# Decode attention with whole-load VectorE instructions: one multiply, half-add and sum per 8 MB K load, and 512-byte aligned buffers

## The chip, the cores and the metric

One core of one Trainium2 chip. The metric is the device time of one execution in microseconds (us), taken as the median of several executions. The span of a profile is about 2 us shorter than the device time. PE is TensorE, DVE VectorE, ACT ScalarE, SP the engine that issues the loads.

## The reference, cut to what matters

Two problems of the same form, A and B: one new token, 32 heads of 128, K and V caches of 16,384 keys. A attends to all keys, B to the last 4,096.

```python
q = (x @ wq).reshape(B, Sq, Hq, Dh)                  # Sq = 1, Hq = Hkv = 32, Dh = 128
scores = einsum("bhqd,bhkd->bhqk", q, k) * Dh**-0.5  # B: k and v are the last 4096 keys
p = softmax(scores); o = einsum("bhqk,bhkd->bhqd", p, v)
return o.reshape(B, Sq, Hq * Dh) @ wo                # the two results are concatenated
```

In bf16 this reads 268 MB of K and V for A, 67 MB for B and 16.8 MB of weights, 352 MB in all, for very little arithmetic.

## The kernel before: the parts that matter

K and V are read in 20 loads of 8 MB each (16 of A, 4 of B, one B load after every four of A). Each of the 128 partitions gets 256 consecutive keys of one head, 64 KB. There are two buffers for K and one for V; all loads are issued in one fixed order (K0, K1, V0, K2, V1, ...), each as soon as its buffer is free. An A load is one "unit" of two heads; a B load is two units of four heads each.

A load of K is worked on in two chunks of 128 keys. DVE multiplies K by q in place, adds the upper half of each key's 128 products to the lower half, PE sums the 64 rest to 8 with matmuls by the identity into PSUM, DVE sums those 8, ACT takes the exp:

```python
def _mult(nc, cx, ch):
    k = u.load.kt[:, ch.k0 : ch.k0 + U, :]                       # U = 128 keys
    cx.o(nc.vector.tensor_tensor(out=k, in0=k, in1=q..., op=ALU.mult))
def _add(nc, cx, ch):
    cx.o(nc.vector.tensor_tensor(out=k[:, :, 0:64], in0=k[:, :, 0:64], in1=k[:, :, 64:128], op=ALU.add))
def _red(nc, cx, ch):                                            # 16 matmuls, 2 PSUM banks
    ch.red = cx.red_pool.tile([P, U, W], F32, tag="red")         # red_pool: 2 buffers
    ...
def _softmax(nc, cx, ch):                                        # DVE sum of 8, then R exps on ACT
    ...
```

P·V runs on PE, one unit at a time, into one of two PSUM accumulators. Then DVE "picks" the wanted rows (a masked multiply, L247, and a sum, L253), and PE folds them into the result. The order in which this is put into the engines' programs (`...` marks cuts):

```python
    def pv(load):
        for u in load.units:
            fin_pe()                   # PE: fold units already picked
            fin_dve()                  # DVE: pick units whose P.V has been issued
            _pv(nc, cx, u)             # PE: P.V
            ...
    for i, x in enumerate(loads):
        for c, ch in enumerate(x.chunks):
            _mult(nc, cx, ch)
            if prev is not None:
                _softmax(nc, cx, prev)
            fin_pe()
            _add(nc, cx, ch)
            fin_dve()
            _red(nc, cx, ch)
            if i and c == 0:
                pv(loads[i - 1])       # P.V of the load before
            prev = ch
```

At the end the output weights wo (8 MB) are loaded into V's buffer, in pieces of which B's last are small, and PE multiplies: 32 matmuls for A, 64 narrower ones for B (`out_ps`).

The 64 KB buffers of this kernel start 256 bytes past a multiple of 512, since the small tiles lie below them.

The softmax here doesn't subtract the row's maximum and nothing guards it: scores larger than these inputs give would overflow.

Of the kernel before, what the change touches and what calls it, by code (L numbers as in the profile page):

```python
# [10 lines left out]
P = 128  # L11
# [4 lines left out]
DH = 128  # L16
U = 128
W = 8
KEYS = 256
# [42 lines left out]

class _Chunk:
    def __init__(self, unit, i):
        self.unit, self.i, self.k0 = unit, i, unit.k0 + i * U


class _Unit:


    def __init__(self, st, i, load, k0):
        self.st, self.i, self.R = st, i, st.R
        self.load, self.k0 = load, k0
        self.h0 = i * st.R
        self.chunks = [_Chunk(self, c) for c in range(st.keys // U)]
        self.stage = None


class _Load:


    def __init__(self, st, i):
        self.st = st
        n = KEYS // st.keys
        self.units = [_Unit(st, i * n + j, self, j * st.keys) for j in range(n)]
        self.chunks = [ch for u in self.units for ch in u.chunks]

# [39 lines left out]
def _q(nc, cx, st):  # L127

    D, N = st.wq.shape
    KC = D // P  # L130
    R = st.R
    n = N // R
    st.qall = cx.singles.tile([P, n], BF16, tag=f"qall{st.name}", name=f"qall{st.name}")
    for j in range(n // 512):
        q_ps = cx.red_pool.tile([P, 512], F32, tag="red", name="q_ps")
        for g in range(R):
            for c in range(KC):
                w = st.wq_t[:, c, :].rearrange("p (u g d) -> p g u d", g=R, d=DH)
                cx.o(nc.tensor.matmul(  # L139
                    q_ps[:, :],  # L140
                    lhsT=st.xb[:, c, g, :],
                    rhs=w[:, g, j * (512 // DH) : (j + 1) * (512 // DH), :],
                    start=(g == 0 and c == 0),
                    stop=(g == R - 1 and c == KC - 1),
                ))
        cx.o(nc.scalar.copy(st.qall[:, j * 512 : (j + 1) * 512], q_ps[:, :]))

# [21 lines left out]

def _mult(nc, cx, ch):  # L170

    u = ch.unit
    k = u.load.kt[:, ch.k0 : ch.k0 + U, :]
    q = u.st.qall[:, u.i * DH : (u.i + 1) * DH]
    cx.o(nc.vector.tensor_tensor(  # L175
        out=k, in0=k,
        in1=q.rearrange("p (o d) -> p o d", o=1).broadcast_to([P, U, DH]),
        op=ALU.mult,
    ))


def _add(nc, cx, ch):
    k = ch.unit.load.kt[:, ch.k0 : ch.k0 + U, :]
    cx.o(nc.vector.tensor_tensor(  # L184
        out=k[:, :, 0 : DH // 2], in0=k[:, :, 0 : DH // 2], in1=k[:, :, DH // 2 : DH], op=ALU.add,
    ))


def _red(nc, cx, ch):
    n = 512 // W  # L190
    nb = DH // 2 // W
    ch.red = cx.red_pool.tile([P, U, W], F32, tag="red", name="red")
    for k in range(0, U, n):
        for b in range(nb):
            cx.o(nc.tensor.matmul(  # L195
                ch.red[:, k : k + n, :],
                lhsT=cx.ident[:, :],
                rhs=ch.unit.load.kt[:, ch.k0 + k : ch.k0 + k + n, b * W : (b + 1) * W],
                start=(b == 0),
                stop=(b == nb - 1),  # L200
            ))
    if ch is ch.unit.load.chunks[-1]:
        cx.loads.release("kt")


def _softmax(nc, cx, ch):

    u = ch.unit
    R = u.R
    sc = cx.sc_pool.tile([P, U], F32, tag="sc", name="sc")  # L210
    cx.o(nc.vector.tensor_reduce(out=sc[:, :], in_=ch.red[:, :, :], axis=AX.X, op=ALU.add))  # L211
    ch.p = u.st.p_pool.tile([P, U // 4, R, 4], BF16, tag=f"p{u.st.name}", name="p_sb")
    for g in range(R):
        cx.o(nc.scalar.activation(  # L214
            out=ch.p[:, :, g, :],
            in_=sc[:, :].rearrange("p (t e) -> p t e", e=4),
            func=ACT.Exp,
            scale=SCALE,
            bias=u.st.off[:, g : g + 1],
            accum_out=u.st.cs[:, u.h0 + g, ch.i : ch.i + 1],  # L220
        ))


def _pv(nc, cx, u):

    R = u.R
    cx.turn = 1 - cx.turn
    u.acc = cx.acc[cx.turn]
    T = u.st.keys // 4
    for t in range(T):  # L230
        r = 32 * (t % 4)
        ch, k = u.chunks[4 * t // U], u.k0 + 4 * t
        cx.o(nc.tensor.matmul(  # L233
            u.acc[r : r + 4 * R, :],
            lhsT=ch.p[:, t % (U // 4), :, :],
            rhs=u.load.vt[:, k : k + 4, :],
            start=(t < 4),
            stop=(t >= T - 4),
        ))
    if u is u.load.units[-1]:  # L240
        cx.loads.release(u.load.v_tag)


def _fin_pick(nc, cx, u):
# [6 lines left out]
    ))  # L251
    u.s = cx.small.tile([P, DH], F32, tag="s", name="s")
    cx.o(nc.vector.tensor_reduce(  # L253
# [15 lines left out]
def _fin_rows(nc, cx, sts):  # L269
    H = 32  # L270
    csum = cx.small.tile([P, 2 * H], F32, tag="csum", name="csum")
    for st in sts:
        cx.o(nc.vector.tensor_reduce(
            out=csum[:, st.f_at : st.f_at + H], in_=st.cs[:, :, :], axis=AX.X, op=ALU.add,
        ))
        cx.o(nc.tensor.matmul(
            cx.f_ps[st.f_at : st.f_at + H, DH : DH + 1],
            lhsT=csum[:, st.f_at : st.f_at + H], rhs=cx.ones_col[:, 0:1],
            start=False, stop=True, skip_group_check=True,
        ))  # L280
# [48 lines left out]
def kernel(  # L329
# [22 lines left out]
    pool = lambda name, bufs, **kw: ctx.enter_context(tc.tile_pool(name=name, bufs=bufs, **kw))  # L352
    PS = dict(space=bass.MemoryType.PSUM)
    cx.singles = pool("singles", 1)
    cx.small = pool("small", 1)
    cx.kt_pool = pool("kt", 2)
    cx.vt_pool = pool("vt", 1)
    cx.accs_pool = pool("accs", 1)
    cx.sc_pool = pool("sc", 1)
    cx.p_poolA = pool("pA", 3)  # L360
    cx.p_poolB = pool("pB", 2)
    cx.red_pool = pool("red", 2, **PS)
    cx.psf_pool = pool("psf", 1, **PS)
# [7 lines left out]
    def problem(name, x, k_cache, v_cache, wq, wo, sk0, W, at):  # L371
# [10 lines left out]
        assert k_cache.shape[1] == 32  # L382
        st.p_pool = cx.p_poolA if name == "A" else cx.p_poolB
        n = KEYS // st.keys * st.R
# [34 lines left out]
    at = (stA.R + stB.R) * (A_wq.shape[0] // P) * P  # L419
    cx.one = cx.singles.tile([1, 1], BF16, tag="one", name="one")  # L420
    nc.gpsimd.memset(cx.one[:, :], 1.0)

    cx.ones_col = cx.singles.tile([P, 1], F32, tag="ones_col", name="ones_col")
    nc.gpsimd.memset(cx.ones_col[:, :], 1.0)
    ones = cx.scr[:, at : at + 3 * P]
    nc.gpsimd.memset(ones, 1.0)
    cx.ident = cx.singles.tile([P, P], BF16, tag="ident", name="ident")
    nc.gpsimd.affine_select(
# [21 lines left out]
    )  # L450

    rows = cx.small.tile([P, 32], F32, tag="rows", name="rows")
    nc.vector.tensor_reduce(
        out=rows[:, :], in_=cx.ident[:, :].rearrange("p (c w) -> p w c", w=32), axis=AX.X, op=ALU.add,
    )
    for st in (stA, stB):
        H, R = 32, st.R
        st.cs = cx.singles.tile([P, H, st.keys // U], F32, tag=f"cs{st.name}", name=f"cs{st.name}")
        own = rows[:, 0 : 4 * R].rearrange("p (g e) -> p g e", e=4)
# [11 lines left out]
    for st in (stA, stB):  # L471
        st.off = cx.singles.tile([P, st.R], F32, tag=f"off{st.name}", name=f"off{st.name}")
        nc.vector.tensor_reduce(
            out=st.off[:, :],
            in_=cx.ident[:, :].rearrange("p (i g) -> p g i", g=st.R),
            axis=AX.X,
            op=ALU.add,
        )
        nc.vector.tensor_scalar(
            out=st.off[:, :], in0=st.off[:, :], scalar1=-1.0, scalar2=1000.0,  # L480
            op0=ALU.add, op1=ALU.mult,
        )
# [17 lines left out]

    fins = []

    def fin_pe():
        for u in fins:
            if u.stage == 1:
                _fin_fold(nc, cx, u)
                u.stage = 9
        fins[:] = [u for u in fins if u.stage != 9]

    def fin_dve():  # L510
        for u in fins:
            if u.stage == 0:
                _fin_pick(nc, cx, u)
                u.stage = 1

    def pv(load):
        for u in load.units:
            fin_pe()
            fin_dve()
            _pv(nc, cx, u)  # L520
            u.stage = 0
            fins.append(u)

    prev = None
    for i, x in enumerate(loads):
        for c, ch in enumerate(x.chunks):
            _mult(nc, cx, ch)
            if prev is not None:
                _softmax(nc, cx, prev)
            fin_pe()  # L530
            _add(nc, cx, ch)
            fin_dve()
            _red(nc, cx, ch)
            if i and c == 0:
                pv(loads[i - 1])
            prev = ch
    _softmax(nc, cx, prev)
    fin_pe()
    fin_dve()
    pv(loads[-1])  # L540
    while fins:
        fin_pe()
        fin_dve()
    _fin_rows(nc, cx, (stA, stB))
# [32 lines left out]
```

## Time and profile before

| | before |
|---|---|
| device time, median of 3 | 823.35 us (823.29 to 824.57) |
| span of the profile | 821.3 us |
| share of 16 DMA engines' span used by the load queue | 99.3% |
| DVE busy, PE busy | 603.5 us (73%), 341.5 us (42%) |

These lines are from the page of the kernel before: busy time of the engines, GB/s moved in 40 slices of the span, the packets and the load queue.

```profile
PE 341.5 (42%) x2148; PEld 127.6 (16%) x2148; DVE 603.5 (73%) x196; ACT 46.8 (6%) x201; POOL 1.3 (0%) x9
...
GB/s 385 436 457 409 456 413 453 411 452 421 427 442 444 425 440 428 437 419 447 421 444 437 431 435 434 432 422 444 440 418 451 425 444 421 445 415 454 413 423 321
DMA packets 8238, 352.65 MB, mean 429 GB/s; under 512 B 916, under 2 KB 920, under 8 KB 1304
...
q1 hardware_dynamic: 8212, 352.33, 99.3%
```

No slice between the first and the last drops: the swings between 409 and 457 come from the bookkeeping, which counts a 64 KB packet whole in the slice in which it starts; by the starts and ends of the packet records no 10 us between 10 and 810 us has engine time lost. The records have a median of 2.418 us per 64 KB packet, 27.1 GB/s per engine and 434 GB/s for 16.

The next view is the chain of waits that ended last, cut to the end of the span (start, length, what). Each line is what released the next.

```profile
756.14 42.58 DMA vt<-in_B_v_cache_dram
...
798.77 3.49 PE acc L233 x31
...
805.50 8.70 PE out_ps L313 x32
...
815.05 3.70 PE out_ps L313 x64
818.75 0.41 DVE rowB L322
```

After the last V has landed, the end is reached through PE's work, not through the wo load. Yet the last packet of wo also lands only at 818.0 us by the packet records: the two end together.

The timeline of SP near the start shows when loads are issued (start, length of the issue):

```profile
75.75 0.54 SPq L167 DMA_DIRECT2D kt<-in_A_k_cache_dram  x1
93.19 0.54 SPq L167 DMA_DIRECT2D vt<-in_A_v_cache_dram  x1
103.48 0.54 SPq L167 DMA_DIRECT2D kt<-in_A_k_cache_dram  x1
124.50 0.53 SPq L167 DMA_DIRECT2D vt<-in_A_v_cache_dram  x1
```

The first line is K2. The loads issued before it (wq, K0, K1, V0) are 33.6 MB, which at 434 GB/s from 1.8 us on last to about 79 us.

### The profile page before, as it was taken

How to read it: one execution, taken by the hardware profiler on the slowest of the kernel's cores; microseconds unless marked ns; L12 is line 12 of the kernel's file. 1: busy time of each engine (PE TensorE's matmuls, PEld its weight loads, DVE VectorE, ACT ScalarE, POOL GpSimd, SP SyncE). 2: the span in 40 equal slices, each digit the busy share in tenths (PEclk: the TensorE clock that was granted, in tenths of full speed). 3: DMA queues.
4: the chain of work that ended last, by engine and by line, in shares of the span. 5: the costliest groups of instructions: out<-in, count | busy, mean ns of one | idle time of the engine just before them, and what ended most of it. 6: DMA issues, size and time to landing. Idle time of an engine off the chain costs nothing.

```text
span 821.3 us, 4921 instructions
## 1 busy us (share of the span) xinstructions
PE 341.5 (42%) x2148; PEld 127.6 (16%) x2148; DVE 603.5 (73%) x196; ACT 46.8 (6%) x201; POOL 1.3 (0%) x9
## 2 busy tenths in 40 slices
PE   3433743435043517162433524344504360715267
PEld 1111211112011202021111211111201120202123
DVE  2099895996469967799169959599556987689911
ACT  1100000000000000001000000000000000000100
POOL 0000000000000000000000000000000000000000
PEclk9856678667676756686757776777767576758678
DMA  9999999999999999999999999999999999999997
GB/s 385 436 457 409 456 413 453 411 452 421 427 442 444 425 440 428 437 419 447 421 444 437 431 435 434 432 422 444 440 418 451 425 444 421 445 415 454 413 423 321
DMA packets 8238, 352.65 MB, mean 429 GB/s; under 512 B 916, under 2 KB 920, under 8 KB 1304
## 3 DMA queue, kind: packets, MB, share of 16 engines
q1 hardware_dynamic: 8212, 352.33, 99.3%
q8 instruction: 17, 0.28, 0.1%
q14 instruction: 5, 0.04, 0.0%
q10 hardware_dynamic: 4, 0.00, 0.0%
HBM read 352.32 MB, written 0.00 MB: 429 GB/s over the span
## 4 chain that ended last, share of the span: by engine, by line
DMA 54%; DVE 22%; PE 15%; issue 8%; SPq 0%; ACT 0%; DVEq 0%
DMA kt<-in_A_k_cache_dram 41%; PE red L195 11%; DVE kt L184 10%; DMA vt<-in_A_v_cache_dram 9%; DVE kt L175 8%; DMA vt<-in_B_v_cache_dram 5%; DVE sc L211 2%; PE acc L233 2%; PE out_ps L313 2%; DVE s L253 0%; DVE acc L247 0%; SPq L124 0%; DVE rowA L322 0%; SPq L167 0%; DVE rowB L322 0%
## 5 line engine op out<-in xcount | busy, mean ns | idle before, releaser
L195 PE MATMUL red<-kt,ident 128*128 128x512 bf16 x640 | 223.3, 526 | 417.7 <-DVE kt L184 417.7
L175 DVE TENSOR_TENSOR kt<-kt,qallA 128x16384 bf16<-128x16384 bf16 x32 | 278.0, 8686 | 135.1 <-DMA kt<-in_A_k_cache_dram 135.1
L184 DVE TENSOR_TENSOR kt<-kt 128x8192 bf16<-128x8192 bf16 x40 | 176.5, 4413 | 0.0
L195 PEld LDWEIGHTS <-ident 128*128 128x128 bf16 x640 | 79.0, 129 | 557.2 <-DVE kt L184 404.8
L233 PE MATMUL acc<-vt,p_sb 128*8 128x512 bf16 (+1 forms) x1280 | 83.0, 416 | 43.0 <-DMA vt<-in_A_v_cache_dram 35.5
L175 DVE TENSOR_TENSOR kt<-kt,qallB 128x16384 bf16<-128x16384 bf16 x8 | 69.5, 8682 | 0.0
L214 ACT ACTIVATE p_sb<-sc,offA 128x128 bf16<-128x128 f32 x64 | 25.2, 394 | 556.8 <-DVE sc L211 556.8
L211 DVE TENSOR_REDUCE sc<-red 128x128 f32<-128x1024 f32 x40 | 48.7, 1216 | 2.2 <-PE red L195 2.2
L233 PEld LDWEIGHTS <-p_sb 128*8 128x8 bf16 (+1 forms) x1280 | 32.3, 93 | 91.8 <-issue 63.0
L247 DVE TENSOR_TENSOR acc<-acc,maskB 128x512 f32<-128x512 f32 x8 | 5.6, 696 | 33.7 <-PE acc L233 33.7
L247 DVE TENSOR_TENSOR acc<-acc,maskA 128x512 f32<-128x512 f32 x16 | 11.1, 692 | 24.9 <-PE acc L233 24.9
L214 ACT ACTIVATE p_sb<-sc,offB 128x128 bf16<-128x128 f32 x32 | 12.4, 390 | 163.7 <-DVE sc L211 163.7
L139 PE MATMUL q_ps<-wq_t,scr 128*128 128x512 bf16 x64 | 16.0, 413 | 5.4 <-DMA wq_t<-in_A_wq_dram 4.8
L253 DVE TENSOR_REDUCE s<-acc 128x128 f32<-128x512 f32 x24 | 16.6, 691 | 1.1
L214 ACT ACTIVATION_READ_ACCUMULATOR p_sb<-sc,offA 128x1 f32 x64 | 11.9, 186 | 0.0
L313 PE MATMUL out_ps<-wo_t,ocA 128*1 128x512 bf16 x32 | 8.7, 438 | 0.3 <-DVE ocA L306 0.3
L139 PEld LDWEIGHTS <-scr 128*128 128x128 bf16 x64 | 6.5, 104 | 14.5 <-issue 7.3
L322 DVE CAST rowA<-out_ps 1x512 bf16<-1x512 f32 x1 | 0.7, 679 | 8.8 <-PE out_ps L313 8.8
L261 PE MATMUL f_ps<-s,selA 128*32 128x128 f32 x32 | 6.5, 285 | 0.0
L214 ACT ACTIVATION_READ_ACCUMULATOR p_sb<-sc,offB 128x1 f32 x32 | 6.0, 186 | 0.0
L111 DVE CAST scr<-xT 128x128 bf16<-128x128 f32 (+1 forms) x6 | 2.1, 460 | 3.8 <-PE xT L103 3.7
L313 PE MATMUL out_ps<-wo_t,ocB 128*1 128x256 bf16 x64 | 3.7, 272 | 0.9 <-DVE ocB L306 0.9
(45 smaller groups left out, 27.5 us busy)
## 6 DMA issues: line engine op xcount, KB each, us to landing
kt<-in_B_k_cache_dram SPq DMA_DIRECT2D x8, 4096.0 KB, 33.2
vt<-in_B_v_cache_dram SPq DMA_DIRECT2D x8, 4096.0 KB, 23.4
wq_t<-in_A_wq_dram SPq DMA_DIRECT2D x1, 4096.0 KB, 12.2
wq_t<-in_B_wq_dram SPq DMA_DIRECT2D x1, 4096.0 KB
wo_t<-in_A_wo_dram SPq DMA_DIRECT2D x2, 2048.0 KB, 22.3
wo_t<-in_B_wo_dram SPq DMA_DIRECT2D x1, 2048.0 KB, 26.6
wo_t<-in_B_wo_dram SPq DMA_DIRECT2D x1, 1024.0 KB, 28.7
wo_t<-in_B_wo_dram SPq DMA_DIRECT2D x1, 512.0 KB
```

The source lines that it names most:

```text
L111: cx.o(nc.vector.tensor_copy(st.xb[:, :, g, :].rearrange("p c (i r) -> p r c i", r=R)[:, g, :, :], xT[:, :].rearrange("p (c o) -> p c o", ...
L139: cx.o(nc.tensor.matmul(q_ps[:, :], lhsT=st.xb[:, c, g, :], rhs=w[:, g, j * (512 // DH) : (j + 1) * (512 // DH), :], start=(g == 0 and c = ...
L175: cx.o(nc.vector.tensor_tensor(out=k, in0=k, in1=q.rearrange("p (o d) -> p o d", o=1).broadcast_to([P, U, DH]), op=ALU.mult,))
L184: cx.o(nc.vector.tensor_tensor(out=k[:, :, 0 : DH // 2], in0=k[:, :, 0 : DH // 2], in1=k[:, :, DH // 2 : DH], op=ALU.add,))
L195: cx.o(nc.tensor.matmul(ch.red[:, k : k + n, :], lhsT=cx.ident[:, :], rhs=ch.unit.load.kt[:, ch.k0 + k : ch.k0 + k + n, b * W : (b + 1) * ...
L211: cx.o(nc.vector.tensor_reduce(out=sc[:, :], in_=ch.red[:, :, :], axis=AX.X, op=ALU.add))
L214: cx.o(nc.scalar.activation(out=ch.p[:, :, g, :], in_=sc[:, :].rearrange("p (t e) -> p t e", e=4), func=ACT.Exp, scale=SCALE, bias=u.st.of ...
L233: cx.o(nc.tensor.matmul(u.acc[r : r + 4 * R, :], lhsT=ch.p[:, t % (U // 4), :, :], rhs=u.load.vt[:, k : k + 4, :], start=(t < 4), stop=(t ...
L247: cx.o(nc.vector.tensor_tensor(out=acc, in0=acc, in1=st.mask[:, :].rearrange("p (x o) -> p x o", o=1).broadcast_to([P, 4, DH]), op=ALU.mult,))
L253: cx.o(nc.vector.tensor_reduce(out=u.s[:, :], in_=acc.rearrange("p x d -> p d x"), axis=AX.X, op=ALU.add,))
L261: cx.o(nc.tensor.matmul(cx.f_ps[st.f_at : st.f_at + 32, 0:DH], lhsT=st.sel[:, at : at + 32], rhs=u.s[:, :], start=(u.i == 0), stop=(u.i == ...
L313: cx.o(nc.tensor.matmul(out[x], lhsT=st.oc[:, j : j + 1], rhs=st.wo_t[:, j, x * w : (x + 1) * w], start=(j == 0), stop=(j == J - 1),))
```

## The change

The intent: fewer and longer DVE and ACT instructions, a simpler order, and K and V buffers on multiples of 512 bytes. A whole K load is multiplied in one instruction (two for B, whose two units have their own q), half-added in one and summed in one; its sums fill four PSUM banks with a single buffer. Only the first two loads are worked on in parts (four and two). A's exps cover 256 keys. Small tiles that must lie low stay below the big buffers, and the rest goes above. The picks of a load now come after both of its P·V units. Core of the diff, cut:

```diff
-def _mult(nc, cx, ch):
+def _mult(nc, cx, load, k0, k1):
+    for u in load.units:
+        a, b = max(k0, u.k0), min(k1, u.k0 + u.st.keys)
...
-    ch.red = cx.red_pool.tile([P, U, W], F32, tag="red", name="red")
+    if k0 == 0:
+        load.red = cx.red_pool.tile([P, KEYS, W], F32, tag="red", name="red")
...
-    cx.singles = pool("singles", 1)
-    cx.small = pool("small", 1)
+    cx.low = pool("low", 1)
     cx.kt_pool = pool("kt", 2)
     cx.vt_pool = pool("vt", 1)
+    cx.singles = pool("singles", 1)
+    cx.small = pool("small", 1)
+    cx.s_pool = pool("s", 2)
...
-    cx.red_pool = pool("red", 2, **PS)
+    cx.red_pool = pool("red", 1, **PS)
...
-    def pv(load):
-        for u in load.units:
-            fin_pe()
-            fin_dve()
-            _pv(nc, cx, u)
...
+    def end(load):
+        for u in load.units:
+            _fin_pick(nc, cx, u)
+        for u in load.units:
+            _fin_fold(nc, cx, u)
...
+        n = KEYS // (4, 2)[i] if i < 2 else KEYS
+        for k in range(0, KEYS, n):
+            _mult(nc, cx, x, k, k + n)
+            if prev is not None and k == 0:
+                _softmax(nc, cx, prev)
+            _add(nc, cx, x, k, k + n)
+            if prev is not None and k == 0:
+                for u in prev.units:
+                    _pv(nc, cx, u)
+            _red(nc, cx, x, k, k + n)
+        if prev is not None:
+            end(prev)
```

More of the change, by code (lines that the diff above doesn't have):

```diff
@@ L16 @@
 DH = 128
-U = 128
 W = 8
@@ L60, in pump @@
             fn()
-class _Chunk:
-    def __init__(self, unit, i):
-        self.unit, self.i, self.k0 = unit, i, unit.k0 + i * U
 class _Unit:
@@ L74, in __init__ @@
         self.h0 = i * st.R
-        self.chunks = [_Chunk(self, c) for c in range(st.keys // U)]
-        self.stage = None
 class _Load:
@@ L85, in __init__ @@
         self.units = [_Unit(st, i * n + j, self, j * st.keys) for j in range(n)]
-        self.chunks = [ch for u in self.units for ch in u.chunks]
 def _load_x(nc, cx, st, w):
@@ L133, in _q @@
     st.qall = cx.singles.tile([P, n], BF16, tag=f"qall{st.name}", name=f"qall{st.name}")
+    q_ps = cx.red_pool.tile([P, n // 512, 512], F32, tag="red", name="q_ps")
     for j in range(n // 512):
-        q_ps = cx.red_pool.tile([P, 512], F32, tag="red", name="q_ps")
         for g in range(R):
@@ L139, in _q @@
                 cx.o(nc.tensor.matmul(
-                    q_ps[:, :],
+                    q_ps[:, j, :],
                     lhsT=st.xb[:, c, g, :],
@@ L145, in _q @@
                 ))
-        cx.o(nc.scalar.copy(st.qall[:, j * 512 : (j + 1) * 512], q_ps[:, :]))
+    cx.o(nc.scalar.copy(st.qall[:, :], q_ps[:, :, :].rearrange("p j f -> p (j f)")))
 def _load_wo(nc, cx, st, j0, n):
@@ L167, in _load_kv, with _add @@
         cx.o(nc.sync.dma_start(out=t[:, u.k0 : u.k0 + st.keys, :], in_=src))
-def _mult(nc, cx, ch):
-    u = ch.unit
-    k = u.load.kt[:, ch.k0 : ch.k0 + U, :]
-    q = u.st.qall[:, u.i * DH : (u.i + 1) * DH]
-    cx.o(nc.vector.tensor_tensor(
-        out=k, in0=k,
-        in1=q.rearrange("p (o d) -> p o d", o=1).broadcast_to([P, U, DH]),
-        op=ALU.mult,
-    ))
-def _add(nc, cx, ch):
-    k = ch.unit.load.kt[:, ch.k0 : ch.k0 + U, :]
+def _mult(nc, cx, load, k0, k1):
+    for u in load.units:
+        a, b = max(k0, u.k0), min(k1, u.k0 + u.st.keys)
+        if a >= b:
+            continue
+        k = load.kt[:, a:b, :]
+        q = u.st.qall[:, u.i * DH : (u.i + 1) * DH]
+        cx.o(nc.vector.tensor_tensor(
+            out=k, in0=k,
+            in1=q.rearrange("p (o d) -> p o d", o=1).broadcast_to([P, b - a, DH]),
+            op=ALU.mult,
+        ))
+def _add(nc, cx, load, k0, k1):
+    k = load.kt[:, k0:k1, :]
     cx.o(nc.vector.tensor_tensor(
@@ L186, in _add, with _red @@
     ))
-def _red(nc, cx, ch):
+def _red(nc, cx, load, k0, k1):
     n = 512 // W
     nb = DH // 2 // W
-    ch.red = cx.red_pool.tile([P, U, W], F32, tag="red", name="red")
-    for k in range(0, U, n):
+    if k0 == 0:
+        load.red = cx.red_pool.tile([P, KEYS, W], F32, tag="red", name="red")
+    for k in range(k0, k1, n):
         for b in range(nb):
             cx.o(nc.tensor.matmul(
-                ch.red[:, k : k + n, :],
+                load.red[:, k : k + n, :],
                 lhsT=cx.ident[:, :],
-                rhs=ch.unit.load.kt[:, ch.k0 + k : ch.k0 + k + n, b * W : (b + 1) * W],
+                rhs=load.kt[:, k : k + n, b * W : (b + 1) * W],
                 start=(b == 0),
@@ L201, in _red, with _softmax @@
             ))
-    if ch is ch.unit.load.chunks[-1]:
+    if k1 == KEYS:
         cx.loads.release("kt")
-def _softmax(nc, cx, ch):
-    u = ch.unit
-    R = u.R
-    sc = cx.sc_pool.tile([P, U], F32, tag="sc", name="sc")
-    cx.o(nc.vector.tensor_reduce(out=sc[:, :], in_=ch.red[:, :, :], axis=AX.X, op=ALU.add))
-    ch.p = u.st.p_pool.tile([P, U // 4, R, 4], BF16, tag=f"p{u.st.name}", name="p_sb")
-    for g in range(R):
-        cx.o(nc.scalar.activation(
-            out=ch.p[:, :, g, :],
-            in_=sc[:, :].rearrange("p (t e) -> p t e", e=4),
-            func=ACT.Exp,
-            scale=SCALE,
-            bias=u.st.off[:, g : g + 1],
-            accum_out=u.st.cs[:, u.h0 + g, ch.i : ch.i + 1],
-        ))
+def _softmax(nc, cx, load):
+    st = load.st
+    R = st.R
+    sc = cx.sc_pool.tile([P, KEYS], F32, tag="sc", name="sc")
+    cx.o(nc.vector.tensor_reduce(out=sc[:, :], in_=load.red[:, :, :], axis=AX.X, op=ALU.add))
+    for u in load.units:
+        n = st.keys
+        u.p = cx.p_pool.tile([P, n // 4, R, 4], BF16, tag="p", name="p_sb")
+        for g in range(R):
+            h = st.f_at + u.h0 + g
+            cx.o(nc.scalar.activation(
+                out=u.p[:, :, g, :],
+                in_=sc[:, u.k0 : u.k0 + n].rearrange("p (t e) -> p t e", e=4),
+                func=ACT.Exp,
+                scale=SCALE,
+                bias=st.off[:, g : g + 1],
+                accum_out=cx.cs[:, h : h + 1],
+            ))
 def _pv(nc, cx, u):
@@ L231, in _pv @@
         r = 32 * (t % 4)
-        ch, k = u.chunks[4 * t // U], u.k0 + 4 * t
+        k = u.k0 + 4 * t
         cx.o(nc.tensor.matmul(
             u.acc[r : r + 4 * R, :],
-            lhsT=ch.p[:, t % (U // 4), :, :],
+            lhsT=u.p[:, t, :, :],
             rhs=u.load.vt[:, k : k + 4, :],
@@ L251, in _fin_pick @@
     ))
-    u.s = cx.small.tile([P, DH], F32, tag="s", name="s")
+    u.s = cx.s_pool.tile([P, DH], F32, tag="s", name="s")
     cx.o(nc.vector.tensor_reduce(
@@ L270, in _fin_rows @@
     H = 32
-    csum = cx.small.tile([P, 2 * H], F32, tag="csum", name="csum")
     for st in sts:
-        cx.o(nc.vector.tensor_reduce(
-            out=csum[:, st.f_at : st.f_at + H], in_=st.cs[:, :, :], axis=AX.X, op=ALU.add,
-        ))
         cx.o(nc.tensor.matmul(
             cx.f_ps[st.f_at : st.f_at + H, DH : DH + 1],
-            lhsT=csum[:, st.f_at : st.f_at + H], rhs=cx.ones_col[:, 0:1],
+            lhsT=cx.cs[:, st.f_at : st.f_at + H], rhs=cx.ones_col[:, 0:1],
             start=False, stop=True, skip_group_check=True,
@@ L353 @@
     PS = dict(space=bass.MemoryType.PSUM)
+    cx.low = pool("low", 1)
+    cx.kt_pool = pool("kt", 2)
+    cx.vt_pool = pool("vt", 1)
     cx.singles = pool("singles", 1)
     cx.small = pool("small", 1)
-    cx.kt_pool = pool("kt", 2)
-    cx.vt_pool = pool("vt", 1)
+    cx.s_pool = pool("s", 2)
     cx.accs_pool = pool("accs", 1)
     cx.sc_pool = pool("sc", 1)
-    cx.p_poolA = pool("pA", 3)
-    cx.p_poolB = pool("pB", 2)
-    cx.red_pool = pool("red", 2, **PS)
+    cx.p_pool = pool("p", 3)
+    cx.red_pool = pool("red", 1, **PS)
     cx.psf_pool = pool("psf", 1, **PS)
@@ L382, in problem @@
         assert k_cache.shape[1] == 32
-        st.p_pool = cx.p_poolA if name == "A" else cx.p_poolB
         n = KEYS // st.keys * st.R
@@ L419 @@
     at = (stA.R + stB.R) * (A_wq.shape[0] // P) * P
-    cx.one = cx.singles.tile([1, 1], BF16, tag="one", name="one")
+    cx.one = cx.low.tile([1, 1], BF16, tag="one", name="one")
     nc.gpsimd.memset(cx.one[:, :], 1.0)
-    cx.ones_col = cx.singles.tile([P, 1], F32, tag="ones_col", name="ones_col")
+    cx.ones_col = cx.low.tile([P, 1], F32, tag="ones_col", name="ones_col")
     nc.gpsimd.memset(cx.ones_col[:, :], 1.0)
@@ L426 @@
     nc.gpsimd.memset(ones, 1.0)
-    cx.ident = cx.singles.tile([P, P], BF16, tag="ident", name="ident")
+    cx.ident = cx.low.tile([P, P], BF16, tag="ident", name="ident")
     nc.gpsimd.affine_select(
@@ L450 @@
     )
+    cx.cs = cx.singles.tile([P, 64], F32, tag="cs", name="cs")
     rows = cx.small.tile([P, 32], F32, tag="rows", name="rows")
@@ L457 @@
         H, R = 32, st.R
-        st.cs = cx.singles.tile([P, H, st.keys // U], F32, tag=f"cs{st.name}", name=f"cs{st.name}")
         own = rows[:, 0 : 4 * R].rearrange("p (g e) -> p g e", e=4)
@@ L471 @@
     for st in (stA, stB):
-        st.off = cx.singles.tile([P, st.R], F32, tag=f"off{st.name}", name=f"off{st.name}")
+        st.off = cx.low.tile([P, st.R], F32, tag=f"off{st.name}", name=f"off{st.name}")
         nc.vector.tensor_reduce(
@@ L499 @@
     ld.release("vt")
-    fins = []
-    def fin_pe():
-        for u in fins:
-            if u.stage == 1:
-                _fin_fold(nc, cx, u)
-                u.stage = 9
-        fins[:] = [u for u in fins if u.stage != 9]
-    def fin_dve():
-        for u in fins:
-            if u.stage == 0:
-                _fin_pick(nc, cx, u)
-                u.stage = 1
-    def pv(load):
-        for u in load.units:
-            fin_pe()
-            fin_dve()
-            _pv(nc, cx, u)
-            u.stage = 0
-            fins.append(u)
+    def end(load):
+        for u in load.units:
+            _fin_pick(nc, cx, u)
+        for u in load.units:
+            _fin_fold(nc, cx, u)
     prev = None
     for i, x in enumerate(loads):
-        for c, ch in enumerate(x.chunks):
-            _mult(nc, cx, ch)
-            if prev is not None:
+        n = KEYS // (4, 2)[i] if i < 2 else KEYS
+        for k in range(0, KEYS, n):
+            _mult(nc, cx, x, k, k + n)
+            if prev is not None and k == 0:
                 _softmax(nc, cx, prev)
-            fin_pe()
-            _add(nc, cx, ch)
-            fin_dve()
-            _red(nc, cx, ch)
-            if i and c == 0:
-                pv(loads[i - 1])
-            prev = ch
-    _softmax(nc, cx, prev)
-    fin_pe()
-    fin_dve()
-    pv(loads[-1])
-    while fins:
-        fin_pe()
-        fin_dve()
+            _add(nc, cx, x, k, k + n)
[5 more added lines that the diff above has]
+            end(prev)
+        prev = x
+    _softmax(nc, cx, prev)
+    for u in prev.units:
+        _pv(nc, cx, u)
+    end(prev)
     _fin_rows(nc, cx, (stA, stB))
```

## The prediction

> **What bounds the kernel now.** The DMA engines, nearly end to end. The profile's queue table has q1 busy for 99.3% of 16 engines' span: 352 MB at 429 GB/s over 821.3 us. In the trace's packet records all 4,096 packets of 64 KB took 2.418 us (27.1 GB/s, 434 GB/s for 16); the large packets sum to 816.1 us per engine, and loads run from 1.8 to 818.6 us, so under 3 us is lost, nearly all at the very end. The Trainium skill (DMA: Bandwidth & Descriptors, Specifications) gives a fabric ceiling of 435 GB/s; the trace agrees. DVE is busy 603.5 us (73%), PE 42%. In the timeline SyncE issues each V 10 to 14 us before the load ahead of it lands: the queue never runs dry.
>
> **What the change does.**
> - DVE: 40 multiplies of 8.68 us become 28, 40 half-adds of 4.41 us become 24, 40 sums of 1.22 us become 20, each longer in proportion; only start costs go, I estimate 0.1 us per merged instruction, some 5 us of 603, off the critical path.
> - ACT: A's 64 exps (0.39 us each) become 32 of 256 keys; off the path.
> - Buffers: K now leaves its buffer as one block. Per load DVE needs about 17.3 (multiply) + 2.4 (sum) + 8.8 (add) + 1.4 or 2.8 (picks) = 30 to 31 us, against the 38.6 us in which DMA brings a K and a V. Counted from K's landing, P·V of the load before ends at about +28 us and its buffer is wanted by +37; the bank sums end at about +40 and K's buffer is wanted by +56. Margins stay positive (9 and 15 us) even at half TensorE clock.
> - Start: one 2,048-column copy behind a single PSUM buffer delays the second Q projection by about 2 us; K1 is issued near 31 us, and the queue holds work till 41. The split first load frees its buffer near 72 us (75.75 before).
> - Alignment: a packet costs about 8 ns beyond its bytes at 27.2 GB/s (2.418 against 1.213 us for half the size). That is all that an aligned start could save, 0.3%; I expect nothing.
> - Tail: the last A load's P·V still waits for its V (779 us). Then come 32 bank sums instead of 16, a 2.4 us sum, eight exps and two P·V units, of which the second needs the last V (798.6) anyway. I put its end 0 to 1.5 us after the 802.3 of before. The output matmuls also need wo, whose last piece lands near 818.5; before, both ended together at 818.7.
>
> **Prediction.** DMA stretch unchanged, tail about +0.5 us: 823.9 us, 80% range 820.5 to 827.5. Faster by over 2%: 0.02; within 2%: 0.95; slower: 0.03.
>
> **What would show each step.** Right: queue share 99% or more, 427 to 431 GB/s, 64 KB packets still 2.41 to 2.42 us; DVE about 590 to 600 us; no stretch in mid-kernel with DMA share clearly under 1; the last P·V ending at 802 to 804 us. Wrong: GB/s dips every 39 us (a buffer came free late), packets under 2.40 us (alignment mattered), or out_ps starting after 808 us.
>
> **What would make it wrong.** A buffer released later than I reckon, because bank sums now queue on TensorE behind a P·V that waits for its V (several us per load, could reach 2%); DVE instructions longer than proportional; a lower granted TensorE clock; packet time depending on alignment after all (up to 2.7 us saved).

## More of the kernel before

DVE's costliest groups, shapes kept apart (count, then busy us and mean ns of one, then idle time just before them):

```profile
L175 DVE TENSOR_TENSOR kt<-kt,qallA 128x16384 bf16<-128x16384 bf16 x32 | 278.0, 8686 | 135.1 <-DMA kt<-in_A_k_cache_dram 135.1
L184 DVE TENSOR_TENSOR kt<-kt 128x8192 bf16<-128x8192 bf16 x40 | 176.5, 4413 | 0.0
...
L211 DVE TENSOR_REDUCE sc<-red 128x128 f32<-128x1024 f32 x40 | 48.7, 1216 | 2.2 <-PE red L195 2.2
...
L247 DVE TENSOR_TENSOR acc<-acc,maskB 128x512 f32<-128x512 f32 x8 | 5.6, 696 | 33.7 <-PE acc L233 33.7
```

DVE is idle for 135 us waiting for K. The last line shows another idle time, 33.7 us before only eight small picks of B, waiting for P·V.

## The result, and the profile after

| | before | after |
|---|---|---|
| device time, median of 4 | 823.84 us | 823.20 us (823.08 to 823.26) |
| ratio | 1 | 0.9991, 95% interval 0.9974 to 1.0009 |
| span of the profile | 821.3 us | 821.2 us |
| load queue's share | 99.3% | 99.3% |
| DVE busy | 603.5 us in 196 instructions | 600.7 us in 146 |
| ACT busy | 46.8 us | 35.1 us |
| PE busy | 341.5 us | 301.1 us |

A ratio here is the mean time of one kernel's runs over that of the other's runs of the same rounds, so it is not quite the ratio of the medians. The page of the kernel after, same lines:

```profile
PE 301.1 (37%) x2148; PEld 117.3 (14%) x2148; DVE 600.7 (73%) x146; ACT 35.1 (4%) x133; POOL 1.3 (0%) x9
...
GB/s 383 434 457 412 456 412 454 412 454 418 427 442 444 425 441 429 441 416 447 421 445 437 431 435 434 432 423 443 441 418 451 425 445 421 448 413 455 413 424 317
DMA packets 8235, 352.62 MB, mean 429 GB/s; under 512 B 916, under 2 KB 920, under 8 KB 1304
...
q1 hardware_dynamic: 8212, 352.33, 99.3%
```

All three engines are busy for less time (PE with the same 2,148 matmuls), and the DMA row is nearly the same, slice by slice. The median packet is again 2.418 us. The chain of waits at the end has changed, though:

```profile
756.43 32.55 DMA vt<-in_B_v_cache_dram
788.99 0.02 issue
789.00 29.16 DMA wo_t<-in_B_wo_dram
818.16 0.04 issue
818.21 0.43 PE out_ps L307 x4
818.63 0.41 DVE rowB L316
```

The chain of before left the DMA engines at 798.8 us, when the last V had landed, and went through PE from there. The chain of after stays with the DMA engines until the last piece of wo lands at 818.2, and only four matmuls follow. DVE's groups:

```profile
L169 DVE TENSOR_TENSOR kt<-kt,qallA 128x32768 bf16<-128x32768 bf16 x14 | 241.2, 17226 | 131.0 <-DMA kt<-in_A_k_cache_dram 131.0
L178 DVE TENSOR_TENSOR kt<-kt 128x16384 bf16<-128x16384 bf16 x18 | 156.3, 8681 | 0.0
...
L206 DVE TENSOR_REDUCE sc<-red 128x256 f32<-128x2048 f32 x20 | 45.7, 2284 | 5.6 <-PE red L190 5.6
...
L245 DVE TENSOR_TENSOR acc<-acc,maskB 128x512 f32<-128x512 f32 x8 | 5.5, 692 | 4.5 <-PE acc L231 4.5
```

A doubled instruction takes 0.146 us less than two single ones (17.226 against 2 x 8.686; the half-add and the sum give 0.145 and 0.148). Neighbours on DVE overlap by about 0.08 us in the timeline, so most of that was never lost: DVE has 50 instructions fewer (48 by merging) and 2.8 us less busy time, under 0.06 us for each. The Trainium skill (Perfetto Trace Analysis, Optimizing Scalar/DVE Operations) puts the data-access overhead of a DVE instruction on SBUF at about 60 ns of engine time, and the latency that the profile shows at about twice that, since the end of one overlaps the next; the two numbers here, 0.146 us of length and under 0.06 us of busy time, are near these (the second is a mean that includes the sums, which read PSUM). The last line is the idle time that I had passed over in before: 4.5 us now, 33.7 then.

The 131.0 us in the first of these lines are the waits before one of three shapes of A's multiply only. These are DVE's waits for A's K before all shapes, and its waits for P·V at the picks of A and B (us in total, times, longest); first before:

```profile
DVE kt L175 <- DMA kt<-in_A_k_cache_dram: 135.1, 13, 31.3
DVE acc L247 <- PE acc L233: 58.6, 9, 9.5
```

then after:

```profile
DVE kt L169 <- DMA kt<-in_A_k_cache_dram: 162.5, 15, 31.5
DVE acc L245 <- PE acc L231: 26.0, 6, 5.9
```

DVE waits 32.6 us less for P·V at the picks and 27.4 us more for A's K: most of what it gains there, it spends waiting for the next load. SP's issues near the start:

```profile
72.44 0.54 SPq L158 DMA_DIRECT2D kt<-in_A_k_cache_dram  x1
88.58 0.54 SPq L158 DMA_DIRECT2D vt<-in_A_v_cache_dram  x1
102.90 0.54 SPq L158 DMA_DIRECT2D kt<-in_A_k_cache_dram  x1
127.32 0.54 SPq L158 DMA_DIRECT2D vt<-in_A_v_cache_dram  x1
```

K2 is issued 3.3 us earlier, by the split of the first load, and V2 2.8 us later. Since the queue has work at all these moments, the packets move as before.

So the question is not why nothing was lost, but what the change was worth, and where that went. My theory: the DMA engines hide it; on DVE it is worth only start costs. Rivals: alignment gained something that coarser blocks lost again; the coarse blocks are only just saved by the split; the change is worth much more than I thought and all of it is hidden.

### The profile page after: what moved, and what is told of

It reads as the page before. It is cut to its first block, busy times and chain, and to the rows that moved or that the text cites. A ratio compares the mean times of both kernels' runs of the same rounds, so it can differ in the third digit from the quotient of the medians.

```text
span 821.2 us, 4767 instructions
## 1 busy us (share of the span) xinstructions
PE 301.1 (37%) x2148; PEld 117.3 (14%) x2148; DVE 600.7 (73%) x146; ACT 35.1 (4%) x133; POOL 1.3 (0%) x9
## 3 DMA queue, kind: packets, MB, share of 16 engines
q1 hardware_dynamic: 8212, 352.33, 99.3%
## 4 chain that ended last, share of the span: by engine, by line
DMA 61%; issue 15%; DVE 13%; PE 11%; ACT 0%; SPq 0%; DVEq 0%
DMA kt<-in_A_k_cache_dram 42%; DMA vt<-in_A_v_cache_dram 12%; PE red L190 7%; DVE kt L178 6%; DVE kt L169 4%; PE acc L231 4%; DMA vt<-in_B_v_cache_dram 4%; DMA wo_t<-in_B_wo_dram 4%; DVE sc L206 2%; ACT p_sb L212 0%; SPq L115 0%; PE out_ps L307 0%; DVE rowB L316 0%; DVEq L169 0%
## 5 line engine op out<-in xcount | busy, mean ns | idle before, releaser
L169 DVE TENSOR_TENSOR kt<-kt,qallA 128x32768 bf16<-128x32768 bf16 (+2 forms) x20 | 276.2, 13810 | 162.5 <-DMA kt<-in_A_k_cache_dram 162.5
L231 PE MATMUL acc<-vt,p_sb 128*8 128x512 bf16 (+1 forms) x1280 | 113.0, 530 | 444.4 <-ACT p_sb L212 344.4
L178 DVE TENSOR_TENSOR kt<-kt 128x16384 bf16<-128x16384 bf16 (+2 forms) x24 | 174.3, 7261 | 0.2
L190 PE MATMUL red<-kt,ident 128*128 128x512 bf16 x640 | 151.2, 396 | 54.6 <-DVE kt L178 54.6
L231 PEld LDWEIGHTS <-p_sb 128*8 128x8 bf16 (+1 forms) x1280 | 37.6, 112 | 515.7 <-ACT p_sb L212 419.8
L190 PEld LDWEIGHTS <-ident 128*128 128x128 bf16 x640 | 63.0, 101 | 142.2 <-issue 47.1
L206 DVE TENSOR_REDUCE sc<-red 128x256 f32<-128x2048 f32 x20 | 45.7, 2284 | 5.6 <-PE red L190 5.6
L212 ACT ACTIVATE p_sb<-sc,offA 128x256 bf16<-128x256 f32 x32 | 16.0, 500 | 574.7 <-DVE sc L206 574.7
L245 DVE TENSOR_TENSOR acc<-acc,maskA 128x512 f32<-128x512 f32 x16 | 11.1, 694 | 21.4 <-PE acc L231 21.4
L212 ACT ACTIVATION_READ_ACCUMULATOR p_sb<-sc,offA 128x1 f32 x32 | 6.0, 187 | 0.0
```

Of the source, the lines that this page charges most:

```text
L169: cx.o(nc.vector.tensor_tensor(out=k, in0=k, in1=q.rearrange("p (o d) -> p o d", o=1).broadcast_to([P, b - a, DH]), op=ALU.mult,))
L178: cx.o(nc.vector.tensor_tensor(out=k[:, :, 0 : DH // 2], in0=k[:, :, 0 : DH // 2], in1=k[:, :, DH // 2 : DH], op=ALU.add,))
L190: cx.o(nc.tensor.matmul(load.red[:, k : k + n, :], lhsT=cx.ident[:, :], rhs=load.kt[:, k : k + n, b * W : (b + 1) * W], start=(b == 0), st ...
L206: cx.o(nc.vector.tensor_reduce(out=sc[:, :], in_=load.red[:, :, :], axis=AX.X, op=ALU.add))
L212: cx.o(nc.scalar.activation(out=u.p[:, :, g, :], in_=sc[:, u.k0 : u.k0 + n].rearrange("p (t e) -> p t e", e=4), func=ACT.Exp, scale=SCALE, ...
L231: cx.o(nc.tensor.matmul(u.acc[r : r + 4 * R, :], lhsT=u.p[:, t, :, :], rhs=u.load.vt[:, k : k + 4, :], start=(t < 4), stop=(t >= T - 4),))
```

## The experiments

Times are medians of 4 or 5 runs; ratios are to the kernel before on the same chip in the same rounds (it ran at 823.0 to 823.3 us there).

### 1. Alignment: a_mis256 and a_mis32

After, with a dummy tile of 256 or of 32 bytes below the big buffers, which moves them up by as much. The results stay right.

```diff
     cx.low = pool("low", 1)
+    cx.pad = cx.low.tile([P, 128], BF16, tag="pad", name="pad")     # a_mis32: [P, 16]
+    nc.gpsimd.memset(cx.pad[:, :], 0.0)
```

> After, with its 64 KB buffers moved up by 256 bytes (256 past a multiple of 512, as in the kernel before). DMA theory (alignment does nothing for packets that stream at the fabric's rate): 64 KB packets 2.418 us again, time 823.2 plus or minus 0.7 us, 0.998 to 1.002 of after. Rival (alignment gained something that the rest of the change lost again): packets of 2.43 us or more, 826 us or more.

> After, with its 64 KB buffers moved up by 32 bytes, off every 256-byte boundary. DMA theory: [...]packets 2.418 to 2.43 us, time 823 to 827 us. Rival (the DMA writes need 512-byte starts): packets clearly over 2.45 us and a time over 830 us.

Measured: a_mis256 823.73 us (823.20 to 823.80), ratio 0.9999 (0.9987 to 1.0012), median packet 2.418 us. a_mis32 825.80 us (825.50 to 826.57), ratio 1.0028 (1.0015 to 1.0040), median packet 2.421 us; in after 4,006 of the 4,096 packets of 64 KB take at most 2.420 us, in a_mis256 4,000, in a_mis32 only 1,100. So moving from 256 bytes past a multiple of 512 to exactly on it, as the change does, is worth nothing that these runs show; starting 32 bytes off it costs about 2.5 us of 823. The Trainium skill (DMA: Bandwidth & Descriptors, How a descriptor splits into AXI transactions) says, of reading, that a transaction has to start on a 256-byte boundary, so that a descriptor which does not start there begins with one from the boundary below, part of it unused; by my count from this rule a 64 KB descriptor then needs one transaction more. The traces agree in kind, 3 ns in the median packet at 32 bytes off and none at 256; but what was moved here is the side that is written, and no offset between 32 and 256 was tried, so the cause is not shown and the runs do not tell a 256-byte grid from one of 64 or 128.

### 2. The split of the first loads: a_nosplit

```diff
-        n = KEYS // (4, 2)[i] if i < 2 else KEYS
+        n = KEYS
```

> After, with its first two K loads processed whole instead of in parts. DMA theory: K0's buffer comes free near 75 us instead of 72, the queue holds work till 80, so no gap; 823.2 us plus or minus 0.7. Rival (the split is what kept the one-block scheme from starving the DMA queue at the start): a gap of 3 us or more near 80 or 100 us, and 826 us or more.

Measured: 824.37 us (823.57 to 824.61), ratio 1.0007 (0.9991 to 1.0022), the same as before within the interval. K2 was issued at 76.80 us, and the packet records show no gap near 80 or 100 us (0.01 us of engine time lost). The large gap of the rival is not there, but the median is half a us above the range that I gave: a small miss. The last piece of wo landed about 1 us later than in after; what delayed it I did not settle. The split is worth at most about a microsecond.

### 3. The tail: a_shortwo and b_shortwo

B's half of wo (4 MB) is not loaded, and B multiplies by A's; B's output is wrong. The DMA work then ends before PE's.

```diff
-    st.wo_t = cx.wo_t[:, st.at // st.DN, :, :]
+    st.wo_t = cx.wo_t[:, 0, :, :]
+    if st.name == "B":
+        return
```

> After, with B's output weights not loaded (B uses A's; B's output is wrong on purpose): 4 MB less at the end of the DMA queue. Theory (after ends its own computing 1.7 us earlier than before, and waits that time for wo): span about 819.5, time 821.4 us, that is 1.7 us under after. Rival (the tail is bound by TensorE alone in both): time as after, 823.2.

> Before, with B's output weights not loaded (B's output is wrong on purpose). Theory (the tail of before is bound by its own computing, which ended with the wo load only by coincidence): 823.3 to 823.8 us, no gain. Rival (before too waits for wo): 1 us or more gained.

Measured: a_shortwo 820.94 us, ratio 0.9970 (0.9957 to 0.9982); b_shortwo 822.74 us (821.51 to 824.32), ratio 0.9990 (0.9977 to 1.0003). The timeline of a_shortwo:

```profile
813.22 3.66 PE L309 MATMUL out_ps<-wo_t,ocB 128*1 128x256 bf16 x64 [0.87 <-DVE ocB L302]
```

and of b_shortwo:

```profile
815.25 3.66 PE L315 MATMUL out_ps<-wo_t,ocB 128*1 128x256 bf16 x64 [0.87 <-DVE ocB L308]
```

With half of wo gone, after gains 2.3 us (820.94 against 823.20; by the ratios to before, 0.9970 and 0.9991, 1.7 us) and before nothing that is clear of noise, though its median lies half a us below the range that I gave. So after really has about 2 us less to do behind the last V (in a_shortwo PE even waits another 0.86 us for A's half of wo). In the full kernel it spends them waiting for wo: there B's 64 matmuls begin at 813.35 us, but they end at 818.6, in four pieces with waits for wo between them. Part of where they come from is seen in the timelines of the full kernels. Before, the last P·V unit:

```profile
798.77 3.46 PE L233 MATMUL acc<-vt,p_sb 128*16 128x512 bf16 x32 [7.44 <-DMA vt<-in_B_v_cache_dram]
```

After, the last two:

```profile
796.44 1.90 PE L231 MATMUL acc<-vt,p_sb 128*16 128x512 bf16 x32 [3.79 <-ACT p_sb L212]
...
798.69 1.90 PE L231 MATMUL acc<-vt,p_sb 128*16 128x512 bf16 x32 [0.34 <-DMA vt<-in_B_v_cache_dram]
```

Both last units begin when the last V has landed, but the one of before follows 7.44 us of idle PE and takes 3.46 us, while the one of after takes 1.90 us. The granted clock between 798 and 801 us was 0.50 in before and 1.00 in after. The Trainium skill (TensorE: Matmul & The Clock Gate, What's actually happening) describes a clock that is halved after an idle window of about 3.4 us and comes back after as long a busy one; the trace agrees for the 7.44 us of before. The 3.79 us of after did not halve it; the page says that the window runs freely, so I take it that so short a gap need not fill one. That was partly luck. The same two units follow the same gap, 3.80 us, in a_mis256 and in a_shortwo, and there the clock was halved, from 797.51 and from 795.98 us, each time for 3.41 us; the 64 matmuls took 5.38 us and ended at 801.8 and 801.1. That is still before the 802.2 and 802.4 of before and b_shortwo: with work on the first unit while the last V was landing, the clock was full again at 800.9 and 799.4 us, in before only at 802.0. How the 2 us divide between this and the output matmuls, no run shows.

### 4. DMA taken out of the way: b_lessv and a_lessv

To see what the change is worth on the engines, both kernels load only a quarter of every V; P·V reads that quarter four times. The result is wrong, the instructions of PE, DVE and ACT keep their number and shapes.

```diff
-        cx.o(nc.sync.dma_start(out=t[:, u.k0 : u.k0 + st.keys, :], in_=src))
+        n = st.keys if which == "kt" else st.keys // 4
+        cx.o(nc.sync.dma_start(out=t[:, u.k0 : u.k0 + n, :], in_=src[:, :, 0:n, :]))
...
-        k = u.k0 + 4 * t
+        k = u.k0 + 4 * t % (u.st.keys // 4)
```

> Before, loading a quarter of every V (P.V reads that quarter four times; wrong result on purpose). 126 MB less is 290 us less of DMA work, which leaves 526 us, under the 603 us of VectorE work. Theory: now VectorE bounds it, about 30 us per A load and 31.4 per B load, start 42 us, end 25 us: 655 to 680 us. If K's buffers come free too late for VectorE: 680 to 720 us.

> After, loading a quarter of every V (wrong result on purpose). Theory: bound by VectorE, which has about 0.3 us less per load than before: 3 to 12 us (0.5 to 1.8%) under the same cut of before. Rival 1 (the one-block order costs by late release of K's buffer, hidden till now): slower than the same cut of before by 10 us or more. Rival 2 (the change saves much that DMA hides): 20 us or more under it.

Measured: b_lessv 686.84 us (686.04 to 688.07), a_lessv 665.65 us (663.84 to 666.97), which is 3.1% or 21 us less, in the same rounds. That is rival 2, not my theory of 3 to 12 us. (b_lessv also missed the 655 to 680 us of my theory; it fell in the range that I had given for K's buffers coming too late, but its trace has one wait for K only, the 31.3 us before the first multiply.) DVE's busy time is 602.0 us in b_lessv and 598.8 in a_lessv, as expected. The difference is in what DVE waits for. The waits of DVE in b_lessv (us in total, times, longest):

```profile
DVE acc L248 <- PE acc L234: 26.1, 5, 8.1
```

and in a_lessv:

```profile
DVE acc L246 <- PE acc L232: 5.6, 2, 5.3
```

The timeline of b_lessv, just after a B load, shows how this wait comes about (lines of ACT and PE weight loads left out):

```profile
353.39 4.41 DVE L185 TENSOR_TENSOR kt<-kt 128x8192 bf16<-128x8192 bf16 x1
...
357.87 6.04 PE L196 MATMUL red<-kt,ident 128*128 128x512 bf16 x16 [9.84 <-DVE kt L185]
363.84 3.63 PE L234 MATMUL acc<-vt,p_sb 128*16 128x512 bf16 x64
365.80 0.70 DVE L248 TENSOR_TENSOR acc<-acc,maskB 128x512 f32<-128x512 f32 x1 [7.99 <-PE acc L234]
```

In a B load the loop over units puts the pick of the first unit into DVE's program before the second unit's P·V is issued, and so before the next chunk's multiply. But PE does P·V only after the 16 bank sums of the chunk whose half-add has just ended. The pick cannot start before both are done, and DVE, which works strictly in program order (the Trainium skill says so in TensorE: Matmul & The Clock Gate, Architectural detail: the array is 16× 32×32, not 1× 128×128), stands still for 8 us with the next multiply ready behind it. Three of the four B loads do this (7.78, 7.99 and 8.09 us); the fourth is the last load. In after P·V comes before the bank sums on PE, and the picks come after both P·V units and behind the whole half-add.

### 5. The same wait in a kernel that loads everything: b_dose_l and a_dose_l

Here nothing is taken from the DMA; DVE is loaded until it bounds. An extra DVE read of 160 of 256 keys of K per load (in before in two halves) finds a maximum that is not used. The results stay right.

```diff
+def _dose(nc, cx, load, k0, k1):
+    n = (k1 - k0) * 160 // KEYS                 # the small doses: 44
+    cx.o(nc.vector.tensor_reduce(
+        out=cx.dose[:, 0:1], in_=load.kt[:, k0 : k0 + n, :], axis=AX.XY, op=ALU.max))
...
+            _dose(nc, cx, x, k, k + n)
             _add(nc, cx, x, k, k + n)
```

> Before plus two VectorE reads of K per load, some 11 us each: 21 us per load, over the slack of 8 to 9. Both theories: slower, VectorE bound, about 50 to 52 us per load, 1060 to 1130 us.

> After plus one VectorE read of K per load, some 21 us. Theory (the change saves only start costs on VectorE, about 0.3 us per load): 3 to 12 us under the same dose of before. Rival (it saves more, hidden by DMA): 20 us or more under it.

Measured: b_dose_l 1121.58 us, a_dose_l 1099.18 us, 22.4 us less, again the rival. DVE is busy 1034.8 and 1029.0 us, and its waits for P·V at the pick come to 25.7 us in b_dose_l and 6.6 us in a_dose_l. The two differences, 5.8 and 19.1 us, make up 24.9; a_dose_l waits 4.3 us more for the bank sums (8.6 against 4.3), which brings it to 20.6 of the 21.4 us between the spans (1119.6 and 1098.2). One flaw, explained in experiment 7: the dose also moves the buffers of before by 32 bytes. Here DVE bounds, and after the first load it never waits for K in either run.

### 6. That one part of the change alone: b_lessv_pick

b_lessv with its chunks left as they are; only the order is changed, and the small pick tile gets a second buffer, without which the second pick would wait for a fold that comes later.

```diff
     def pv(load):
+        fin_pe()
+        fin_dve()
         for u in load.units:
-            fin_pe()
-            fin_dve()
             _pv(nc, cx, u)
...
+    cx.s_pool = pool("s", 2)
```

> Before with a quarter of every V loaded (wrong result on purpose, as in the earlier pair), and one thing of the change alone: in a B load both P.V units are issued before VectorE is asked to pick the first one's rows. In the earlier pair before was 21 us slower, VectorE's waits for P.V at the pick were 26.1 us against 5.6, its busy time 602.0 against 598.8. Theory (those waits are the gain that DMA hides, long blocks give some 3 us): 664 to 671 us, waits for P.V at the pick under 8 us, busy time still 602. Rival (the gain comes from working in whole loads): 680 us or more.

Measured: 663.13 us (662.46 to 663.99), ratio to before 0.8059 (0.8046 to 0.8073), where a_lessv has 0.8080 (0.8064 to 0.8096) and b_lessv 0.8338. DVE's waits:

```profile
DVE acc L248 <- PE acc L234: 2.3, 2, 1.5
```

The median lies 0.9 us below the range that I gave. DVE's busy time is 601.7 us, as in b_lessv, and so is PE's (338.0; b_lessv 337.0, a_lessv 299.4), so PE's shorter busy time in after is not the cause. Three lines of order, with the second pick buffer that they need, bring all of what the whole change brings in this pair, where DVE is the bound; with the dose I did not run the order alone. The long instructions, the four-bank sums and the aligned buffers add nothing that can be seen beside it: a_lessv's DVE is busy 2.9 us less than that of b_lessv_pick, but waits 3.3 us more at the picks (5.6 against 2.3) and 0.8 more for the bank sums (5.9 against 5.1).

### 7. How much slack there is: b_dose_s and a_dose_s

The same dose with 44 of 256 keys: 6.0 us more DVE work per load, 120 us in all, less than the 8 us per load by which DVE's work is shorter than the DMA's.

> Before plus two VectorE reads of K per load, some 3 us each (the result stays right): 6 us per load, 120 us in all on VectorE. DMA theory (8 to 9 us of slack per load): time within 1 us of before. Rival (VectorE bounds some stages at 73% busy): 10 us or more added.

> After plus one VectorE read of K per load, some 6 us: 120 us in all on VectorE. DMA theory: within 1 us of after. Rival (the one-block order has used up the slack, so a buffer comes free too late): 5 us or more added.

Measured: b_dose_s 830.89 us, ratio 1.0090 (1.0075 to 1.0105); a_dose_s 831.99 us (828.56 to 833.27), ratio 1.0098 (1.0074 to 1.0121). Both expectations of the DMA theory, "within 1 us", failed: 8 or 9 us of 120 came through. That of a_dose_s is even in the range of its rival ("5 us or more"), but not by the rival's path: late buffers left only 0.8 us of gaps in its DMA queue. The 8 or 9 us came through at the two ends. Before and b_dose_s from 76 to 84 us (length, busy time of PE, PE's loads, DVE, ACT and POOL, clock, DMA share, GB/s); first before:

```profile
76.00:84.00 8.00, 0.57 (x2) 0.28 (x3) 8.00 (x4) 0.88 (x4) 0.00 (x0) 0.65 0.93 401
```

then b_dose_s:

```profile
76.00:84.00 8.00, 5.68 (x16) 1.88 (x14) 8.00 (x1) 0.00 (x0) 0.00 (x0) 0.71 0.72 270
```

In b_dose_s K2 is issued at 81.72 us instead of 75.75, after the queue has run empty: 3.0 us of engine time are lost there and 0.7 more near 100 us. The rest of its loss is a flaw of my experiment: the dose's result tile of 32 bytes lies below the big buffers in the kernel before, so they start 32 bytes off a multiple of 256, and the median packet is 2.421 us as in a_mis32. The packets take about 3 us longer in all, in part those right after the gap. In a_dose_s the buffers stay where they were. It loses under 1 us at the head and most of the rest at the tail, as the chain of waits shows:

```profile
785.38 8.70 DVE kt L185
794.13 9.08 PE red L197 x32
...
815.81 8.47 PE out_ps L314 x32
...
825.14 3.70 PE out_ps L314 x64
```

The chain now goes through DVE's half-add of the last load, delayed by the doses, and PE's sums: the output matmuls start at 815.8 instead of 803.7 us, and no longer wait for wo. In the middle neither kernel lost more than 0.1 us of engine time in any 10 us (a_dose_s apart from 0.4 us near 130 to 150 us), so of the slack of about 8 us per load at least the 6 us that were tried are real there. At the head it is 4 us in before, and at the tail of after the slack that experiment 3 shows is about 2 us.

## Why the prediction was right or wrong, point by point

**The DMA engines bound the kernel, and the stretch of loads is unchanged: right.** The queue's share is 99.3% in both, GB/s agree slice by slice to within 4, the packet is 2.418 us in both. Experiment 4 shows it from the other side: with fewer bytes the same instructions end 137 to 158 us sooner.

**Predicted 823.9 us, measured 823.2: inside the range, with two errors below it that did not matter.**

**Alignment brings nothing: right**, and now shown (experiment 1). Of the offsets tried only 32 bytes cost anything; the kernel before, 256 bytes past a multiple of 512, lost nothing by it.

**"only start costs go": wrong.** This step of the cost of DVE missed the in-order wait. The busy time fell by 2.8 us (I said some 5, at 0.1 us per merged instruction; it was under 0.06), but when DVE bounds, the change is worth 21 to 22 us, nearly all of it because the picks moved behind both P·V units. The group list of before had that line, 33.7 us idle before eight picks of B, and I had counted busy times only. It did not hurt the forecast because DVE has more idle time than that while it waits for K, and these waits grew by 27.4 us when those for P·V fell by 32.6: the gain is off the critical path.

**The buffers come free in time: right in the middle, and I gave no margin for the ends.** For the load that landed at 721.3 us, P·V of the load before ended at 747.9 (+27; predicted +28), and the bank sums at 756.4 (+35; predicted +40). "Margins stay positive (9 and 15 us)" holds for those loads; experiment 7 shows the smallest margin at K2, about 4 us in before. The split of the first load raised it to about 7 us (issue at 72.4), as predicted.

**The tail costs about +0.5 us, the last P·V ending at 802 to 804: wrong in the step, small in effect.** It ended at 800.6 (798.69 + 1.90), earlier than the 802.2 of before, because PE had its full clock there; I had put both units at half clock. In a_mis256, where the clock was halved for 3.41 us, it ended at 801.8, still below my range. Experiment 3 shows that about 2 us are there, and that the wait for wo takes them back. That this error did not show in the time is partly luck: I had named the need for wo, but its last piece lands at about 818 us in both kernels, just when the tail of before happens to end.

**DVE about 590 to 600 us: just missed**, 600.7.

What stays open: the last microsecond of a_nosplit; which grid the alignment needs; and whether long blocks alone, without the new order of the picks, would cost or gain a microsecond or two when DVE bounds. No run did that part alone. No version here that loads everything is clearly faster than both kernels: 352 MB at 434 GB/s are 812 us of the 821, and the reference needs all of these bytes.

## What to carry to other kernels

In a kernel that streams at 99% of its DMA engines, a change of compute that still frees the buffers in time can be worth something only at the head, where the queue is shortest, and behind the last load; look there first, and expect "same" elsewhere. Read idle times as well as busy times when you cost a change: an instruction that waits for another engine in the middle of an in-order program holds up all the work behind it, and a change of order may be worth more than merging instructions. To learn what a hidden change is worth, take the bound away from both kernels, or load the hidden engine until it bounds, and compare; and check that the probe does not move the buffers.

## What the Trainium skill lacked or had wrong

- DMA: Bandwidth & Descriptors, Specifications, gives about 27 GiB/s per engine. The traces show 65,536 bytes in 2.418 us, which is 27.1 GB/s or 25.2 GiB/s; only with GB does the row agree with the page's own ceiling of 435 GB/s for 16 engines, to which this kernel comes within 0.4% (434 GB/s).
- The same page, How a descriptor splits into AXI transactions, has the rule, but no measured cost of an unaligned start for a long transfer. Buffers 32 bytes off a multiple of 256 took 2.421 instead of 2.418 us per 64 KB packet in the median and about 2.5 us more for 352 MB (ratio 1.0028); 256 bytes off a multiple of 512 cost nothing (ratio 0.9999, 0.9987 to 1.0012).
- Perfetto Trace Analysis, Optimizing Scalar/DVE Operations, has larger operations as the remedy for a saturated engine. In these runs, with VectorE saturated, merging took some 3 us off its busy time and nothing visible off the run, while the order of the instructions alone brought some 23 us (ratios to before 0.8059 against 0.8338): this section has no word on an in-order engine that stands still at one early wait. Another section of the page, Optimization Strategy, does send the reader to the gaps on the engine and to what blocks it, which is the step that I left out when I predicted.
